# The rest of the largest expert in a mixture-of-experts kernel: first layer with the weights held in the array instead of the tokens

## The chip, the core and the metric

The kernel runs on one core of one Trainium2 chip. A core has TensorE (PE: matrix products, with its weight loads shown apart as PEld), VectorE (DVE), ScalarE (ACT), GpSimd (POOL), SyncE (SP) and 16 DMA engines. The metric is the device time of one execution in microseconds; lower is better.

## The reference

An attention-like first part (no softmax, with a decay mask) makes `x`, 4608 tokens of 512 numbers. A router picks for each token one of 4 groups and in the group one of 4 experts, 16 in all, and each expert is a two-layer network on its own tokens:

```
xg = x[mask_g]
e_idx = np.argmax(xg @ w_expert[g], axis=1)
...
h = np.maximum(xg[mask_e] @ w1[g, e], 0.0)      # [n, 512] @ [512, 1024]
ye = h @ w2[g, e]                               # [n, 1024] @ [1024, 512]
out[tok_idx] = combined[:, None] * ye
```

With the inputs that the reference draws, the two largest experts have 330 tokens each and the smallest 235.

## The kernel before

The attention part fills the first quarter of the span and stores each token's row, with its weight, into a DRAM table `xs` by expert. Then come 17 passes `p`, in the order of the experts' sizes. Pass 0 takes the first 256 tokens of the largest expert (`EARLY`), passes 1 to 15 one expert each, and pass 16 (`E`), which this case is about, the rest of the largest expert: room for 128 tokens (`CS[E]`), of which 330 - 256 = 74 are used.

All 32-bit operands are split in two: `wh` and `xTh` are the rounded part (`fp32r`), `wl` and `xTl` what is left, and a product is three products, high by high, high by low, low by high. A weight piece is a quarter of an expert's first layer or of its second (512 KB each; `load_piece`); `split(k)` makes `wh` on ACT and `wl` on DVE, two instructions each on 128 x 512. Pieces of pass 16 have the numbers `k0` to `k0 + 7`, even ones of the first layer, odd ones of the second.

Passes 1 to 15 go by eight steps `f` of 128 hidden units. `layer1(p, f)` (L593) keeps a 128 x 128 block of weights in the array and streams the tokens past it, 12 matmuls. `layer2(p, f)` (L998 to L1000) does the same, 12 matmuls into four PSUM tiles `py`. `by_width` puts both into a test of the expert's token count on PE: the smaller of two stream lengths is taken where the count allows it (`LOWS[p]`, else `CS[p]`), and both are in the program, behind a branch (L213). Pass 15 streams 238 columns, pass 14 streams 252.

Pass 16 stands behind the loop and is written out by hand. Its first layer (`last1`, L1052) keeps 128 tokens of one 128-row slice of `xT` in the array and streams 256 weight columns: 12 matmuls for each of four pieces. That leaves the hidden units along the free dimension, so `last_tr` (L1063) transposes each piece with two matmuls, after ACT has put it through the ReLU (`hn`), and ACT and DVE split the result into `hhn` and `hln`. Its second layer (`layer2` with `natural(p)`, L987) keeps 128 tokens of `hhn` or `hln` in the array and streams 512 columns of `w2`, three matmuls for each `f`, all into one PSUM tile that has the place of pass 15's `py_0`. `finish` copies this tile on ACT and stores it with one indirect DMA from POOL; `yturn` and `ystore` do the same for pass 15 in eight transposes on DVE and eight DMAs.

Every engine runs its instructions in the order in which the code issues them. `xturn` and `xsplit` make `xTh` and `xTl` of the next pass on DVE and ACT.

Of the kernel before, what the change touches and what calls it, by code (L numbers as in the profile page):

```python
# [7 lines left out]
F32 = mybir.dt.float32  # L8
F32R = mybir.dt.float32r
BF16 = mybir.dt.bfloat16  # L10
I32 = mybir.dt.int32
AF = mybir.ActivationFunctionType
ALU = mybir.AluOpType
AX = mybir.AxisListType

P = 128
# [4 lines left out]
E = G * EG  # L21
NP = H // 2
NKC = DM // P
NFC = F // P
CAPS = [384, 356, 342, 330, 322, 314, 310, 304, 298, 292, 288, 284, 280, 274, 266, 256]
LOWS = [0, 332, 324, 316, 308, 302, 296, 294, 286, 282, 278, 272, 268, 260, 252, 238]
CMAX = CAPS[0]
EARLY = 256
PICK = 26
# [6 lines left out]
NS = N + P  # L36
NT = N // P
NPIECE = 4
# [27 lines left out]
def moe_retention(ctx, tc, qk, kv, wgt, w1, w2, c_f, out):  # L66
# [55 lines left out]
    pe = nc.tensor  # L122
# [35 lines left out]
    def load_piece(i, parts=(0, 1)):  # L158
        if i < len(pieces):
            raws.setdefault(i, []).extend(wload(*pieces[i], part) for part in parts)  # L160
# [9 lines left out]
    def split(k):  # L170
        split_piece(k // 2, k % 2)
# [29 lines left out]
    def width_of(p):  # L201

        wide[p] = nc.values_load(
            sizes[0:1, p : p + 1], engines=[mybir.EngineType.PE], min_val=0, max_val=NS,
            skip_runtime_bounds_check_because="a count of rows, compared only",
        )

# [720 lines left out]
    def rank_experts():  # L928

        key = sm.tile([P, E], F32, name="key")  # L930
        dve.scalar_tensor_tensor(key, cnt, float(E), eid, ALU.mult, ALU.subtract)
        for j in range(2):
            dve.scalar_tensor_tensor(
                key, eah[j], float((2 - j) * BIG), key, ALU.mult, ALU.add
            )
        kk = sm.tile([P, E, E], F32, name="kk", bufs=1)
        ks3 = [P, E, E]
        dve.tensor_tensor(
            kk, key.unsqueeze(1).to_broadcast(ks3), key.unsqueeze(2).to_broadcast(ks3), ALU.is_gt
        )  # L940
        rk = sm.tile([P, E], F32, name="rk")
        dve.tensor_reduce(rk, kk, AX.X, ALU.add)
        dve.tensor_tensor(
            req, rk.unsqueeze(1).to_broadcast(ks3), eid.unsqueeze(2).to_broadcast(ks3), ALU.is_equal
        )
        dve.tensor_tensor(kk, req, eid.unsqueeze(1).to_broadcast(ks3), ALU.mult)
        with nc.allow_low_precision("integers below 16"):
            dve.tensor_reduce(order, kk, AX.X, ALU.add)
        yield

        cr = sm.tile([P, E], F32, name="cr")
        dve.tensor_tensor(kk, req, cnt.unsqueeze(1).to_broadcast(ks3), ALU.mult)
        dve.tensor_reduce(cr, kk, AX.X, ALU.add)
        dve.tensor_copy(sizes[:, 2:], cr[:, 2:])
        dve.tensor_tensor(
            kk[:, :, 0:NB], slb.unsqueeze(1).to_broadcast([P, E, NB]),
            cr.unsqueeze(2).to_broadcast([P, E, NB]), ALU.is_ge,
        )
        dve.tensor_scalar(mia, kk[:, :, 0:NB], float(BIG), None, ALU.mult)
        yield  # L960
        cb, ce = [sm.tile([P, E], F32, name=f"c{x_}", bufs=1) for x_ in "be"]
        dve.tensor_scalar(cb, cr, sln[:, 0:1], None, ALU.add)
        dve.tensor_tensor(ce, cb, cf[:, KC_CAPB : KC_CAPB + E], ALU.is_ge)
        dve.scalar_tensor_tensor(cb, ce, float(E * NS), cb, ALU.mult, ALU.add)
        dve.tensor_copy(ce, order)
        dve.scalar_tensor_tensor(pads, ce, float(NS), cb, ALU.mult, ALU.add)
        el = sm.tile([P, 3], F32, name="el")
        dve.tensor_scalar(el, sln, float(EARLY), None, ALU.add)
        dve.tensor_scalar(mil, el, cr[:, 0:1], float(BIG), ALU.is_ge, ALU.mult)


    def layer2(p, f):
# [33 lines left out]
    def yturn(p, dc, part=0, of=1):  # L1006

        nb = nblocks(p)
        b0, b1 = nb * part // of, nb * (part + 1) // of
        if dc == 0 and part == 0:  # L1010
            ys[p] = mp.tile([P, NB, DQ], F32, name=f"y_{p}", tag="y", bufs=2)
        dve.transpose(
            ys[p][:, b0:b1, 32 * dc : 32 * dc + 32],
            pys[p][dc][:, 32 * b0 : 32 * b1].rearrange("p (b t) -> p b t", t=32),
        )
# [9 lines left out]
    def finish(p, i):  # L1025
# [11 lines left out]
            out_offset=bass.IndirectOffsetOnAxis(ap=iis[p][:n, i : i + 1], axis=0),  # L1037
            in_=y[:n], in_offset=None, bounds_check=N - 1, oob_is_err=False,
        ))

    hns = {}

    def last1(pc):

        wh, wl = wsp[E * NPIECE + pc, 0]
        xh, xl = xTs[E]
        C = CS[E]
        ph = ps_sm.tile([P, 2 * P], F32, name=f"phn_{pc}", tag="sm")
        n = 0
        for kc in range(NKC):  # L1050
            for a, b in ((xh, wh), (xl, wh), (xh, wl)):
                pe.matmul(  # L1052
                    ph[:C], a[:, kc, :C], b[:, kc, :], start=n == 0, stop=n == 3 * NKC - 1
                )
                n += 1
        hns[pc] = mp.tile([P, 2 * P], F32, name=f"hn_{pc}", tag="hn")
        act.activation(hns[pc][:C], ph[:C], AF.Relu)

    def last_tr(pc):
        C = CS[E]  # L1060
        pt = (ps_tr, ps_st)[pc % 2].tile([P, 2, P], F32, name=f"pth_{pc}", tag="tr")
        for i in range(2):
            pe.transpose(pt[:, i, :C], hns[pc][:C, i * P : (i + 1) * P], ident[:C, :C])  # L1063
        hh = mp.tile([P, CMAX], F32R, name=f"hhn_{pc}", tag="hh", bufs=4)
        hl = mp.tile([P, CMAX], F32R, name=f"hln_{pc}", tag="hl", bufs=4)
        hv, lv = [x_[:, : 2 * C].rearrange("p (i c) -> p i c", i=2) for x_ in (hh, hl)]
        act.copy(hv, pt[:, :, :C])
        dve.tensor_tensor(lv, pt[:, :, :C], hv.bitcast(F32), ALU.subtract)
        for i in range(2):
            hts[E, 2 * pc + i] = (hh[:, i * C : (i + 1) * C], hl[:, i * C : (i + 1) * C])  # L1070

    prev = None
    ranks = rank_experts()
    for p in range(E):
        for f in range(NFC):
# [68 lines left out]
                next(ranks, None)  # L1144
            if (p, f) == (0, 6):
                expert_of(2)
            if f == NFC - 3 and p < E - 1:
                width_of(p + 1)
            if (p, f) == (1, 1):
                ids(1)  # L1150
# [17 lines left out]
                ovt = overflow_tables(*ov, mp, phs, cnt, cf, req, ident, ones, pe, dve)  # L1168
            if p in (2, 3):
                next(ovt, None) if (p, f) >= (2, 3) else None  # L1170
            if f == NFC - 3 and p:
                for i in range(3):
                    xturn(p + 1, i, 3)
            if f == NFC - 2 and p:
                for kc in range(NKC):
                    xsplit(p + 1, kc)
            if f == NFC - 1 and 0 < p < E - 1:
# [5 lines left out]


    k0 = 2 * E * NPIECE
    load_piece(E * NPIECE + 3)
    layer2(*prev)
    for part in range(2):
        for dc in range(NKC):
            yturn(E - 1, dc, part, 2)  # L1190
    for b in range(NB):
        ystore(E - 1, b)
    split(k0 + 4)
    last1(0)
    last1(1)
    last_tr(0)
    split(k0 + 6)
    split(k0 + 3)
    last1(2)
    last_tr(1)  # L1200
    layer2(E, 0)
    layer2(E, 1)
    split(k0 + 5)
    last1(3)
    last_tr(2)
    ids(E)
    split(k0 + 7)
    layer2(E, 2)
    layer2(E, 3)
    last_tr(3)  # L1210
    for f in range(4, NFC):
        layer2(E, f)
    finish(E, 0)
    in_order.close()
# [265 lines left out]
```

## Time and profile before

| what | value |
|---|---|
| time, median of 3 runs | 584.69 us (582.01 to 585.03) |
| profiled execution: its time and its span | 583.33 us, 581.5 us |
| PE busy | 565.8 us, 97% of the span, 6045 matmuls |
| PEld busy | 531.1 us, 91% |
| DVE, ACT, POOL busy | 73%, 56%, 44% |
| mean granted clock of TensorE | 0.998 |

The span runs from the first to the last instruction of the profiled execution; its time is 1.8 us more. Busy shares are means over stages with different limits. A matmul's end is modelled, so of PE the starts are what can be read: how far they are apart is what a matmul costs in a stream of them.

### The profile page before, as it was taken

To read this page: it belongs to the slowest core of one execution; us is meant where nothing else is said; L and a number is where in the kernel's file an instruction comes from. 1 tells how busy PE (TensorE), PEld (TensorE's weight loads), DVE (VectorE), ACT (ScalarE), POOL (GpSimd) and SP (SyncE) were. 2 spreads that over 40 slices of the span, in tenths; PEclk is the share of its full clock that TensorE was granted. 3 is DMA by queue.
4 is the path that set the end of the run, shared out by engine and by line. 5 is a ranking of instruction groups with operands and counts; after the bars stand their busy time and mean duration, and the time that the engine had idled before them with its cause. 6 is when DMAs were issued, how large, how long until landed. Compare 5 with 4: busy or idle time off the path is not lost.

```text
span 581.5 us, 16813 instructions
## 1 busy us (share of the span) xinstructions
PE 565.8 (97%) x6045; PEld 531.1 (91%) x6045; DVE 423.7 (73%) x997; ACT 325.8 (56%) x849; POOL 256.5 (44%) x391
## 2 busy tenths in 40 slices
PE   7998999999999999999999999999999999999995
PEld 5887787877768999999999999999999999999994
DVE  4886777878668668876767675867768687687774
ACT  5687877876346545454545454445545455455564
POOL 0022323323323037463645537383644736538465
PEclk9999999999999999999999999999999999999999
DMA  8998998956977952938375665839385684856851
GB/s 327 406 406 320 333 385 300 361 195 187 360 243 295 253 234 63 332 83 311 81 306 155 243 200 195 279 112 342 82 313 160 232 275 141 327 150 243 278 218 42
DMA packets 62410, 141.98 MB, mean 244 GB/s; under 512 B 9425, under 2 KB 30297, under 8 KB 62304
## 3 DMA queue, kind: packets, MB, share of 16 engines
q1 hardware_dynamic: 52944, 120.19, 59.1%
q0 software_dynamic: 9216, 20.28, 9.8%
q8 instruction: 73, 1.20, 0.8%
q14 instruction: 33, 0.27, 0.1%
q10 hardware_dynamic: 144, 0.05, 0.0%
HBM read 120.22 MB, written 24.81 MB: 249 GB/s over the span
## 4 chain that ended last, share of the span: by engine, by line
PE 88%; DVE 4%; DMA 2%; issue 2%; ACT 1%; POOL 1%; SPq 1%; POOLq 0%; DVEq 0%
PE ph L593 33%; PE py L998 11%; PE py L1000 11%; PE py L999 11%; PE px L793 5%; PE pss L749 3%; PE pxt L363 3%; PE px L811 2%; PE pst L778 2%; PE ph L579 2%; PE plt L405 1%; PE py L987 1%; DMA xb<-xs 1%; DMA b<-in_kv 1%; PE pss L737 1%
## 5 line engine op out<-in xcount | busy, mean ns | idle before, releaser
L117 POOL DMA_INDIRECT out<-y,ii x151 | 164.5, 1089 | 62.7 <-issue 30.8
L117 DVE TENSOR_TENSOR wl<-r,wh 128x512 fp32r<-128x512 f32 x260 | 167.4, 685 | 5.5 <-ACT wh L117 2.4
L117 ACT ACTIVATE hh<-ph 128x256 fp32r<-128x256 f32 (+15 forms) x128 | 53.7, 420 | 201.0 <-PE ph L593 136.6
L117 ACT CAST wh<-r 128x512 fp32r<-128x512 f32 x260 | 147.0, 617 | 0.0
L593 PE MATMUL ph<-xTh_m,wh 128*128 128x324 f32 (+16 forms) x488 | 144.9, 297 | 0.0
L593 PE MATMUL ph<-xTl_m,wh 128*128 128x324 f32 (+16 forms) x488 | 144.4, 296 | 0.1
L593 PE MATMUL ph<-xTh_m,wl 128*128 128x324 f32 (+16 forms) x488 | 144.4, 296 | 0.0
L998 PE MATMUL py<-hh,wh 128*128 128x320 f32 (+19 forms) x480 | 142.5, 297 | 0.0
L1000 PE MATMUL py<-hl,wh 128*128 128x332 f32 (+14 forms) x480 | 141.9, 296 | 0.0
L999 PE MATMUL py<-hh,wl 128*128 128x332 f32 (+14 forms) x480 | 141.8, 295 | 0.0
L117 DVE SCALAR_TENSOR_TENSOR hl<-ph,hh 128x256 fp32r<-128x256 f32 (+14 forms) x122 | 57.0, 467 | 95.9 <-ACT hh L117 95.2
L593 PEld LDWEIGHTS ph<-xTl_m,wh 128*128 128x128 f32 x488 | 92.1, 189 | 0.7 <-DVE xTl_m L117 0.4
L593 PEld LDWEIGHTS ph<-xTh_m,wh 128*128 128x128 f32 x488 | 92.1, 189 | 0.4 <-issue 0.2
L593 PEld LDWEIGHTS ph<-xTh_m,wl 128*128 128x128 f32 x488 | 92.2, 189 | 0.0
L999 PEld LDWEIGHTS py<-hh,wl 128*128 128x128 f32 x480 | 90.7, 189 | 0.0
L998 PEld LDWEIGHTS py<-hh,wh 128*128 128x128 f32 x480 | 90.6, 189 | 0.0
L1000 PEld LDWEIGHTS py<-hl,wh 128*128 128x128 f32 x480 | 90.4, 188 | 0.0
L117 POOL COPY pace<-hh 1x1 f32<-1x1 f32 x140 | 30.0, 214 | 132.7 <-ACT hh L117 123.3
L117 POOL DMA_INDIRECT xs<-xt,sl x33 | 32.7, 992 | 109.9 <-DVE xT L117 39.9
L117 ACT ACTIVATE vs<-b,cf 128x64 f32<-128x64 f32 x288 | 72.4, 336 | 7.1 <-DMA b<-in_kv 5.7
L117 DVE TENSOR_TENSOR sT<-pss,masks 128x512 f32<-128x512 f32 x72 | 46.0, 681 | 14.0 <-PE pss L749 7.7
L793 PE MATMUL px<-sT,vs 128*64 128x128 f32 x576 | 39.9, 279 | 0.8 <-issue 0.4
(194 smaller groups left out, 613.0 us busy)
## 6 DMA issues: line engine op xcount, KB each, us to landing
r<-in_w SPq DMA_DIRECT2D x138, 512.0 KB, 7.5
a<-in_qk SPq DMA_DIRECT2D x35, 512.0 KB, 6.4
b<-in_kv SPq DMA_DIRECT2D x31, 512.0 KB
xb<-xs SPq DMA_DIRECT2D x20, 165.0 KB, 3.6
xb<-xs SPq DMA_DIRECT2D x20, 148.5 KB, 3.3
out<-y,ii POOLq DMA_INDIRECT x151, 2.7
xb<-xs SPq DMA_DIRECT2D x12, 181.5 KB, 5.6
b<-in_kv SPq DMA_DIRECT2D x6, 256.0 KB
```

The lines of the kernel that those rows point to most:

```text
L117: i_ = f(*a, **k)
L363: pe.transpose(T["pxt"][:, i, :], T["xT"][:, i, :], ident)
L405: pe.matmul(plt[32 * i : 32 * i + 32], wgp[:, i, :], tiles[t]["xTg"][:, i], start=True, stop=True)
L579: pe.matmul(ph[:, :C], raws[i][0][:, kc, cs], xTf[p][:, kc, :C], start=kc == 0, stop=kc == NKC - 1)
L593: pe.matmul(ph[:, :w], a[:, kc, cs], b[:, kc, :w], start=n == 0, stop=n == 3 * NKC - 1)
L749: pe.matmul(pss[k_, o, (i + par) * P + late * D : (i + par) * P + to], T["kT"][r, i + par, k_], T["qT"][r, i + par, late * D : to], start= ...
L778: pe.matmul(pst[o * D : o * D + D, i, :], T["k"][:, h, :], T["vs"][:, h, :], start=first and i == 0, stop=True, skip_group_check=True,)
L793: pe.matmul(px[g * D : g * D + D, o, s * P : s * P + P], T["vs"][:, 4 * s + 2 * g + o, :], T["sT"][:, o, 2 * s + g, :], start=s == 0, stop ...
L811: pe.matmul(px[g * D : g * D + D, o, s * P + r * w : s * P + r * w + w], st[rows, 2 * s + g, :], T["qT"][rows, 2 * s + g, r * w : r * w + ...
L998: pe.matmul(py[:, :w0], wh[:, f % 2, ds_], hh[:, :w0], start=st_, stop=False)
L999: pe.matmul(py[:, :w], wl[:, f % 2, ds_], hh[:, :w], start=False, stop=False)
L1000: pe.matmul(py[:, :w], wh[:, f % 2, ds_], hl[:, :w], start=False, stop=sp_)
```

## The change

Pass 16 calls the general `layer1` for its first layer: 128 x 128 weights stay in the array and the tokens stream past, 80 columns where the count allows it and 128 else (`LOWS` has a 17th entry, 80). `last1` and `last_tr` go, with the transposes, `hn`, `hhn` and `hln`. The count for the test is 256 less than that of the largest expert, made by one more DVE instruction early on and read by PE in step 5 of pass 15. `xturn` and `xsplit` of pass 16 go from steps 5 and 6 of pass 15 to steps 2 and 3. A second load of the last two weight pieces, which the loop had loaded already, goes. The order behind the loop is written anew.

```
-LOWS = [0, 332, 324, ..., 252, 238]
+LOWS = [0, 332, 324, ..., 252, 238, 80]
...
+        dve.tensor_scalar(sizes[:, 0:1], cr[:, 0:1], float(-EARLY), 0.0, ALU.add, ALU.max)
...
-    def last1(pc):
...
-                pe.matmul(
-                    ph[:C], a[:, kc, :C], b[:, kc, :], start=n == 0, stop=n == 3 * NKC - 1
-                )
...
-    def last_tr(pc):
...
-            pe.transpose(pt[:, i, :C], hns[pc][:C, i * P : (i + 1) * P], ident[:C, :C])
...
-            if f == NFC - 3 and p < E - 1:
+            if f == NFC - 3:
                 width_of(p + 1)
...
-            if f == NFC - 3 and p:
+            if f == (2 if p == E - 1 else NFC - 3) and p:
                 for i in range(3):
                     xturn(p + 1, i, 3)
-            if f == NFC - 2 and p:
+            if f == (3 if p == E - 1 else NFC - 2) and p:
                 for kc in range(NKC):
                     xsplit(p + 1, kc)
...
     k0 = 2 * E * NPIECE
-    load_piece(E * NPIECE + 3)
+    split(k0 + 3)
     layer2(*prev)
-    for part in range(2):
-        for dc in range(NKC):
-            yturn(E - 1, dc, part, 2)
+    for dc in range(NKC):
+        yturn(E - 1, dc, 0, 2)
+    layer1(E, 0)
+    for dc in range(NKC):
+        yturn(E - 1, dc, 1, 2)
     for b in range(NB):
         ystore(E - 1, b)
+    layer1(E, 1)
     split(k0 + 4)
-    last1(0)
-    last1(1)
-    last_tr(0)
+    layer1(E, 2)
+    layer2(E, 0)
+    layer1(E, 3)
     split(k0 + 6)
-    split(k0 + 3)
-    last1(2)
-    last_tr(1)
-    layer2(E, 0)
     layer2(E, 1)
+    layer1(E, 4)
     split(k0 + 5)
-    last1(3)
-    last_tr(2)
+    layer2(E, 2)
+    layer1(E, 5)
     ids(E)
+    layer2(E, 3)
     split(k0 + 7)
-    layer2(E, 2)
-    layer2(E, 3)
-    last_tr(3)
-    for f in range(4, NFC):
+    layer1(E, 6)
+    layer2(E, 4)
+    layer1(E, 7)
+    for f in range(5, NFC):
         layer2(E, f)
     finish(E, 0)
```

On PE, the end of one piece's first layer and what follows it. In a row the streamed operand stands first and the one held in the array second; the shape is that of the stream. Before:

```order
L1052 MATMUL phn_12299<-wh_16_2_12244,xTh_m_12043 128x256
L1052 MATMUL phn_12299<-wh_16_2_12244,xTl_m_12044 128x256
L1052 MATMUL phn_12299<-wl_16_2_12245,xTh_m_12043 128x256
L1063 MATMUL pth_12314<-cf,hn_12278 128x128 x2
L987 MATMUL py_0_12321<-wh_16_0_12082,hhn_12283 128x512
L987 MATMUL py_0_12321<-wl_16_0_12083,hhn_12283 128x512
L987 MATMUL py_0_12321<-wh_16_0_12082,hln_12284 128x512
```

The same place with the change; the rows with 80 columns repeat four times, and 12 rows with 128 columns stand behind the branch.

```order
L213 COMPARE_AND_BRANCH
L593 MATMUL ph_3519<-xTh_m_11840,wh_16_2_12308 128x80
L593 MATMUL ph_3519<-xTl_m_11841,wh_16_2_12308 128x80
L593 MATMUL ph_3519<-xTh_m_11840,wl_16_2_12309 128x80
...
L988 MATMUL py_0_12343<-wh_16_1_12186,hh_3_12347 128x512
L988 MATMUL py_0_12343<-wl_16_1_12187,hh_3_12347 128x512
L988 MATMUL py_0_12343<-wh_16_1_12186,hl_3_12373 128x512
```

Tokens and weights have changed places in the first layer, and the transposes between the layers are gone; the second layer's rows are the same but for their order.

On DVE, behind pass 15: `wl` is the low half of a weight split, `y` pass 15's result on its way out of `py`, `hl` and `hln` the low half of the hidden layer. Before:

```order
L117 TENSOR_TENSOR wl_16_1_12152<-r_16_1_11767,wh_16_1_12151 128x512 x2
L117 STREAM_TRANSPOSE y_12211<-py_0_11730 128x4x32
L117 STREAM_TRANSPOSE y_12211<-py_1_11731 128x4x32
...
L117 TENSOR_TENSOR wl_16_2_12245<-r_16_2_11907,wh_16_2_12244 128x512 x2
L117 TENSOR_TENSOR hln_12284<-pth_12280,hhn_12283 128x256
L117 TENSOR_TENSOR wl_16_3_12288<-r_16_3_12049,wh_16_3_12287 128x512 x2
```

With the change:

```order
L117 TENSOR_TENSOR wl_16_1_12156<-r_16_1_11768,wh_16_1_12155 128x512 x2
L117 TENSOR_TENSOR wl_16_1_12187<-r_16_1_11770,wh_16_1_12186 128x512
L117 STREAM_TRANSPOSE y_12217<-py_0_11731 128x4x32
L117 STREAM_TRANSPOSE y_12217<-py_1_11732 128x4x32
L117 STREAM_TRANSPOSE y_12217<-py_2_11733 128x4x32
L117 STREAM_TRANSPOSE y_12217<-py_3_11734 128x4x32
L117 SCALAR_TENSOR_TENSOR hl_0_12248<-ph_3474,hh_0_12222 128x128
L117 STREAM_TRANSPOSE y_12217<-py_0_11731 128x4x32
L117 SCALAR_TENSOR_TENSOR hl_1_12305<-ph_3519,hh_1_12279 128x128
L117 TENSOR_TENSOR wl_16_2_12309<-r_16_2_11922,wh_16_2_12308 128x512
```

A split of a second-layer piece (`k0 + 3`) now stands ahead of the transposes of `y`, and one instruction on the hidden layer between their two halves.

## Rows read from the trace of the kernel before

**Rows 1.** The page: busy time and share of the span of PE and its weight loads, and the 40 slices of PE and of the granted clock.

```profile
PE 565.8 (97%) x6045; PEld 531.1 (91%) x6045; DVE 423.7 (73%) x997; ACT 325.8 (56%) x849; POOL 256.5 (44%) x391
PE   7998999999999999999999999999999999999995
PEclk9999999999999999999999999999999999999999
```

**Rows 2.** The last stages and two early ones: us from the span's start, length, then for each engine busy us (instructions), the granted clock, DMA share and GB/s.

```profile
4.00:8.00 4.00, 3.35 (x30) 2.50 (x30) 2.23 (x8) 2.01 (x8) 0.00 (x0) 1.00 0.99 358
8.00:12.00 4.00, 2.76 (x45) 2.21 (x44) 2.60 (x5) 2.28 (x9) 0.00 (x0) 1.00 1.04 423
540.00:563.00 23.00, 23.00 (x205) 23.00 (x204) 17.87 (x39) 13.33 (x31) 13.01 (x18) 1.00 0.82 304
563.00:569.00 6.00, 6.00 (x48) 5.78 (x47) 4.78 (x14) 3.33 (x10) 4.13 (x4) 1.00 0.12 38
569.00:575.30 6.30, 6.30 (x36) 5.12 (x34) 4.53 (x11) 3.46 (x9) 4.71 (x5) 1.00 0.13 43
575.30:581.50 6.20, 0.01 (x1) 0.00 (x0) 0.00 (x0) 0.58 (x1) 0.97 (x1) 0.79 0.09 32
```

**Rows 3.** The chain of work that ended last, pieces from 537 us on: start, length, engine, output and line, how many instructions.

```profile
537.28 1.40 PE ph L593 x12
...
548.31 1.35 PE ph L593 x12
...
563.17 2.87 PE phn L1052 x24
566.04 0.22 PE pth L1063 x2
566.25 1.43 PE phn L1052 x12
567.69 0.22 PE pth L1063 x2
567.90 1.39 PE py L987 x6
```

**Rows 4.** The timeline of PE in order of time: start, length, instruction. First a matmul of pass 14 and one of pass 15, then the first matmul and the last of pass 16.

```profile
537.12 0.28 PE L593 MATMUL ph<-xTh_m,wh 128*128 128x252 f32 x1
...
548.15 0.27 PE L593 MATMUL ph<-xTh_m,wh 128*128 128x238 f32 x1
...
563.01 0.28 PE L1052 MATMUL phn<-wh,xTh_m 128*128 128x256 f32 x1
...
574.91 0.40 PE L987 MATMUL py<-wh,hln 128*128 128x512 f32 x1
```

**Rows 5.** Weight loads by shape over the whole span: partitions times columns of the block that is loaded, type, count, then busy us and mean ns of one.

```profile
L405 PEld LDWEIGHTS plt<-xT,wgp 128*32 128x32 f32 x96 | 1.9, 108 | 1.8 <-issue 1.7
L749 PEld LDWEIGHTS pss<-a 64*64 64x64 f32 x896 | 22.3, 133 | 4.8 <-issue 3.7 <-DVE sT L117 0.6
L363 PEld LDWEIGHTS pxt<-cf,xT 128*128 128x128 f32 x144 | 15.3, 140 | 3.5 <-issue 1.3
L593 PEld LDWEIGHTS ph<-xTh_m,wh 128*128 128x128 f32 x488 | 92.1, 189 | 0.4 <-issue 0.2
```

**Rows 6.** The timeline of the weight loads at four places where a load did not wait for the matmul ahead of it to begin: behind a stall, behind a stall, behind two transposes, and behind two transposes.

```profile
177.86 0.19 PEld L987 LDWEIGHTS py<-wh,hh 128*128 128x128 f32 x1 [0.18 <-ACT hh L117]
177.96 0.19 PEld L987 LDWEIGHTS py<-wl,hh 128*128 128x128 f32 x1
...
178.79 0.19 PEld L987 LDWEIGHTS py<-wh,hl 128*128 128x128 f32 x1 [0.64 <-DVE hl L117]
178.90 0.19 PEld L987 LDWEIGHTS py<-wh,hh 128*128 128x128 f32 x1
...
565.99 0.19 PEld L1052 LDWEIGHTS phn<-wh,xTh_m 128*128 128x128 f32 x1
566.09 0.19 PEld L1052 LDWEIGHTS phn<-wh,xTl_m 128*128 128x128 f32 x1
...
572.29 0.19 PEld L987 LDWEIGHTS py<-wh,hhn 128*128 128x128 f32 x1
572.40 0.19 PEld L987 LDWEIGHTS py<-wl,hhn 128*128 128x128 f32 x1
```

**Rows 7.** The timelines of DVE, ACT, POOL and the DMA queue of SP around the end of pass 15 and of pass 16: start, length, instruction, in brackets the idle time ahead of it and what ended it.

```profile
561.49 1.30 DVE L117 TENSOR_TENSOR wl<-r,wh 128x512 fp32r<-128x512 f32 x2
562.77 1.71 DVE L117 STREAM_TRANSPOSE y<-py 128x128 f32<-128x128 f32 x8
...
560.85 2.17 ACT L117 CAST wh<-r 128x512 fp32r<-128x512 f32 x4
575.35 0.58 ACT L117 COPY y<-py 128x512 f32<-128x512 f32 x1 [2.38 <-PE py L987]
...
563.96 0.96 POOL L117 DMA_INDIRECT out<-y,ii  x1 [4.43 <-DVE y L117]
...
573.96 0.97 POOL L117 DMA_INDIRECT out<-y,ii  x1 [0.30 <-issue]
576.21 0.97 POOL L117 DMA_INDIRECT out<-y,ii  x1 [1.28 <-ACTq L1297]
...
540.75 8.94 SPq L117 DMA_DIRECT2D r<-in_w  x12
```

**Rows 8.** DVE's and ACT's groups by shape from 540 to 576 us: count, busy us, mean ns of one, idle time ahead.

```profile
L117 DVE TENSOR_TENSOR wl<-r,wh 128x512 fp32r<-128x512 f32 x28 | 17.9, 684 | 0.6
L117 DVE SCALAR_TENSOR_TENSOR hl<-ph,hh 128x256 fp32r<-128x256 f32 x8 | 3.4, 424 | 4.6 <-ACT hh L117 4.5
L117 DVE TENSOR_TENSOR xTl_m<-xTf,xTh_m 128x128 fp32r<-128x128 f32 x4 | 0.9, 283 | 0.0
...
L117 ACT ACTIVATE hh<-ph 128x256 fp32r<-128x256 f32 x8 | 3.1, 384 | 9.7 <-PE ph L593 7.0 <-POOL pace L117 1.3 <-issue 1.3
L117 ACT CAST xTh_m<-xTf 128x128 fp32r<-128x128 f32 x4 | 0.9, 298 | 0.0
```

More of the change, by code (lines that the diff above doesn't have):

```diff
@@ L25 @@
 CAPS = [384, 356, 342, 330, 322, 314, 310, 304, 298, 292, 288, 284, 280, 274, 266, 256]
-LOWS = [0, 332, 324, 316, 308, 302, 296, 294, 286, 282, 278, 272, 268, 260, 252, 238]
+LOWS = [0, 332, 324, 316, 308, 302, 296, 294, 286, 282, 278, 272, 268, 260, 252, 238, 80]
 CMAX = CAPS[0]
@@ L203, in width_of @@
         wide[p] = nc.values_load(
-            sizes[0:1, p : p + 1], engines=[mybir.EngineType.PE], min_val=0, max_val=NS,
+            sizes[0:1, p % E : p % E + 1], engines=[mybir.EngineType.PE], min_val=0, max_val=NS,
             skip_runtime_bounds_check_because="a count of rows, compared only",
@@ L1039, in finish @@
         ))
-    hns = {}
-    def last1(pc):
[L1045 to L1051, printed above, removed]
-                pe.matmul(
-                    ph[:C], a[:, kc, :C], b[:, kc, :], start=n == 0, stop=n == 3 * NKC - 1
-                )
-                n += 1
-        hns[pc] = mp.tile([P, 2 * P], F32, name=f"hn_{pc}", tag="hn")
-        act.activation(hns[pc][:C], ph[:C], AF.Relu)
-    def last_tr(pc):
-        C = CS[E]
-        pt = (ps_tr, ps_st)[pc % 2].tile([P, 2, P], F32, name=f"pth_{pc}", tag="tr")
-        for i in range(2):
-            pe.transpose(pt[:, i, :C], hns[pc][:C, i * P : (i + 1) * P], ident[:C, :C])
[L1064 to L1070, printed above, removed]
     prev = None
```

## The prediction

> **What bounds the kernel now.** I read the page first: PE is busy for 97% of the span, its weight loads for 91%, and the slices of PE are full to the end [rows 1]. Then the last stages: between 540 and 575.3 us PE has no idle time, and DVE and ACT, which feed it, are busy for 13.3 and 17.9 of 23 us, then for 8 to 9 and for 7 of 12.3 us [rows 2]. The chain of work that ended last says the same: up to the end of pass 16 it runs on PE, matmul behind matmul [rows 3]. Behind PE comes a tail of 6.2 us (575.3 to 581.5) with one ACT copy and one store from POOL [rows 2, 7]. POOL was free at 574.93 and waited 1.28 us for that copy, so POOL does not set the tail; PE's last matmul does. So the change is worth what it does to PE between 563.01 (the first matmul of pass 16) and the last one at 574.91 [rows 4].
>
> **What a matmul costs there.** From the chain: 24 `phn` of 256 columns take 2.87 us, 0.1196 each; two transposes 0.22; six `py` of 512 columns 1.39, 0.232 each [rows 3]. Pass 16 before is 48 x 0.1196 = 5.74, 8 x 0.11 = 0.88 and 24 x 0.232 = 5.56, in sum 12.18 us; the starts give the same (574.91 + 0.23 - 563.01 = 12.13).
>
> **What the change adds and removes on PE.** The second layer keeps its 24 matmuls: 5.56 us. The first layer's 48 + 8 instructions (6.62 us) become 8 x 12 = 96 matmuls, each with a block of 128 x 128 weights of its own and 80 columns to stream: the 74 tokens fit the smaller width. The streamed columns fall from 48 x 256 + 8 x 128 = 13,312 to 7,680, but the loads rise from 56 to 96. So the question is what 96 matmuls cost that load 128 columns and stream 80. No row of before has this shape in the split 32-bit type.
>
> From below: by the stream alone. 512 columns cost 0.232 and 256 cost 0.1196, so 0.00044 a column, and 80 columns would cost 0.1196 - 176 x 0.00044 = 0.042 us.
>
> From above: a load takes 0.189 us from start to end [rows 5]; if nothing of it lay beside other work, a matmul would cost that, 0.189.
>
> Between them stand the rows on the loads themselves. A 32-bit load takes 108 ns for 32 columns, 133 for 64, 189 for 128 [rows 5]: 25 ns for 32 more, 56 for 64 more, so some 100 to 112 ns of the 189 grow with the columns, and the rest is a delay that the next load can share. The four places of [rows 6] show exactly that. Normally a load starts as the matmul ahead of it starts, and one can't see what the load alone needs. At these four it starts later than that, because the load before it is in the way, and there two loads start 0.10, 0.11, 0.10 and 0.11 us apart, while each takes 0.19. The streams are no counter-example: 252 columns cost 1.40 / 12 = 0.1167 and 238 cost 1.35 / 12 = 0.1125 [rows 3, 4], never under what the loads need. I read it so: loads of 128 columns of 32 bits can't follow each other faster than some 0.105 us, pass 15 already runs just above that, and a shorter stream buys nothing more. I take 0.109, halfway between the 0.105 of the loads and the 0.1125 that was seen in a long stream.
>
> So 96 x 0.109 = 10.46, with the second layer 16.02, against 12.18: **PE needs 3.84 us more.** With 0.10 it is 2.98 more, with 0.1125 it is 4.18.
>
> **A rule of the skill against the row.** The Trainium skill, "TensorE: Matmul & The Clock Gate", section "Back-to-back issue gap", gives about 81 ns a matmul for a sustained stream of load and matmul at 128 columns. By it the first layer would take 96 x 0.081 = 7.8 us and pass 16 some 1.2 us more than now. Against it, for this type, stand [rows 6]; what it would do here is the first rival's upper part.
>
> **What else moves, costed at nothing.** *Splits.* ACT and DVE must deliver, and PE is slower now, so they have time. Walked through with a split at 1.13 us on ACT (four casts took 2.17 [rows 7]) and 1.29 on DVE, a hidden layer at no more than 0.38 and 0.42 [rows 8]: DVE ends `wl` of `k0 + 2` at 562.79 [rows 7], of `k0 + 3` at 564.1, the first half of `y` (four of the eight transposes, 0.86) at 564.9, `hl_0` at 565.3, the second half at 566.2. The first `py` of pass 16 needs that PSUM tile and is due behind three first layers, at 563.01 + 36 x 0.109 = 566.9: 0.7 us to spare. The next splits: `k0 + 4` is ready at 567.9 and due at 569.6, `k0 + 6` at 571.2 and due at 573.6, `k0 + 5` at 573.2 and due at 574.9, `k0 + 7` at 575.2 and due at 577.6. If one comes late, PE waits by that much; nothing else is behind it but the end. *Steps 2 and 3 of pass 15* get the turn and split of pass 16's tokens: step 3 has `hl` 0.42, `wl` 1.29 and four `xTl` 0.89 on DVE, 2.6 of the 2.70 us that a step takes on PE (twice 1.35 [rows 3]), and ACT 0.38 + 1.13 + 0.90. It is what step 6 has now without a gap on PE, and `hl` is needed only one first layer (1.35 us) later. Uncovered it would cost 0.9. *Loads.* Two loads of 512 KB go, the last of twelve issued from 540.75 on [rows 7]. DMA is at 0.12 of its time behind 563 [rows 2], PE waits for none of them: nothing. The pieces are all issued before 550 as before. *Tests.* Eight more tests of the width on PE and one more read of a count. Each step of pass 15 has two of them and PE has no gap there [rows 2]: nothing. *Stores.* POOL's eight stores of pass 15 start about 1 us later (564.9 for 563.96), take 11 us and end near 576, and the last store is due behind 579.7: nothing. The tail behind PE stays at 6.2 us.
>
> **The sum** goes against the profiled execution's own time: 583.33 + 3.84 = 587.2. That execution was 1.4 us under the median of the three runs and inside their spread; from the median it is 588.5. I forecast the middle, **587.9 us**. What a measurement of this kernel tells from no change is about 0.5%, 2.9 us; 3.84 is 0.66%.
>
> **Rivals.**
>
> *The loads hide (not slower).* The loads of [rows 6] may be late for another reason, and short streams let them run faster; the transposes speak for it, whose loads take 140 ns for the same 128 columns [rows 5]. At 0.042 a matmul, PE reaches the first `py` at 563.01 + 36 x 0.042 = 564.5, but DVE frees the tile only at 566.2: a wait of 1.6 us takes part of the gain. 4.03 + 5.56 + 1.6 = 11.2, 1.0 us less than now: 582.3 to 583.7. At 0.081 it is 13.3 and a wait of 0.3, 1.4 us more: 584.8 to 586.1. The point from which it decides is the distance of two loads: below 0.1 us the change is not slower by 0.5%. Against it stand all four places. 0.11.
>
> *Load and stream don't overlap at 80 columns (much slower).* A load that waits until the short stream is out: 0.109 + 0.042 = 0.15 a matmul, 14.4 in all, 7.8 us more: 591 to 592.5; with the whole 0.189, 18.1 and 11.5 more: 595 to 596. Against it: matmuls and loads lie beside each other in every long stream. 0.05.
>
> *The granted clock falls in pass 16.* The array would stream for some 0.03 to 0.04 of every 0.109 us. The mean granted clock was 0.79 behind the last matmul, where PE did nothing [rows 2], so idle time does lower it to 1.2 from 2.4 GHz; but it stayed at 1.00 where PE had nothing in flight for 0.65 and 1.24 of 4 us [rows 2]. No row has matmuls of this type at the lower level; with everything on PE twice as long the bound is 16 us, 604. 0.04.
>
> **Chances.** My forecast 0.80, the hidden loads 0.11, no overlap 0.05, the clock 0.04. Most of the forecast's own spread is that of the runs, 1.5 us to each side, so some of it falls under the 2.9 us: slower 0.70, within 0.5% 0.27, faster 0.03 (the hidden loads at their best, with a low median). The likeliest case alone holds 586.3 to 588.9; the range for 8 in 10, with the spread of the runs and a part of the rivals, is 585.0 to 591.0.
>
> **What would show it.** In the changed kernel, pass 16's `ph` on L593 with 80 columns start 0.108 to 0.112 us apart, 12 in about 1.31 us, and each load starts as the one ahead is through; PE's stretch from the first matmul of pass 16 to the last grows from 12.1 to about 16 us without a gap, and the tail behind it stays at 6.2. Wrong would be: `ph` less than 0.1 us apart; a gap on PE before the first `py` that DVE's `y` ends; a gap in steps 3 to 5 of pass 15; a granted clock under 1.00 ahead of the last matmul.

## The result and the profile after

The changed kernel is slower: the ratio of its times to those of the kernel before, measured on the same chip, is **1.0073, 95% interval 1.0050 to 1.0096** (14 executions of each). On the 583.17 us median of before in that comparison this is +4.3 us, where +3.84 was predicted. Of the 14 executions of the changed kernel, 4 took 597 to 602 us at a mean granted clock of 0.971 to 0.978: the ratio leaves them out, the median of all 14, 589.16 us (584.65 to 602.07), holds them, and E4, E5 and E8 to E10 are about them. The profiled execution took 585.17 us, its span 583.4.

The page after: busy time of PE and its loads, and the 40 slices of PE and of the granted clock, for [rows 1].

```profile
PE 567.6 (97%) x6085; PEld 533.8 (92%) x6085; DVE 424.5 (73%) x1002; ACT 325.3 (56%) x849; POOL 256.1 (44%) x391
PE   7998999999999999999999999999999999999995
PEclk9999999999999999999999999999999999999999
```

Forty more matmuls (6085 for 6045) and no other sign: at this distance the two pages look alike. The windows cut at the first and behind the last matmul of pass 16 show the difference, first of before, then of the changed kernel (columns as in [rows 2]).

```profile
540.00:563.01 23.01, 23.01 (x206) 23.01 (x205) 17.88 (x40) 13.34 (x31) 13.01 (x18) 1.00 0.82 304
563.01:575.14 12.13, 12.13 (x82) 10.89 (x80) 9.30 (x24) 6.79 (x17) 8.84 (x8) 1.00 0.13 41
575.14:581.50 6.36, 0.17 (x1) 0.00 (x0) 0.00 (x0) 0.58 (x1) 0.97 (x1) 0.79 0.09 31
```

```profile
540.00:560.76 20.76, 20.76 (x187) 20.76 (x185) 16.45 (x36) 12.44 (x29) 13.05 (x18) 1.00 0.73 276
560.76:577.04 16.28, 16.28 (x122) 15.04 (x120) 10.19 (x28) 6.32 (x16) 8.44 (x8) 1.00 0.10 33
577.04:583.40 6.36, 0.17 (x1) 0.00 (x0) 0.00 (x0) 0.59 (x1) 0.97 (x1) 0.80 0.08 29
```

PE is busy without a gap in both, from 540 us on and through pass 16. Pass 16 takes 16.28 for 12.13 us, **+4.15**, and the tail behind it 6.36 in both. The whole span is only 1.9 us longer, because in this one execution pass 16 began 2.25 us earlier, at 560.76 for 563.01. The program ahead of that point moves by as much from one execution to the next: in the traces of this case, pass 16 began between 560.8 and 566.1 us. So kernels are compared here by the stretch of pass 16, and by the ratio of many times.

The chain of work that ended last, for [rows 3]: the 36 matmuls of three first layers, one piece's second layer, the next first layer, its second layer.

```profile
560.92 3.95 PE ph L593 x36
564.87 0.78 PE py L988 x3
565.65 1.26 PE ph L593 x12
566.91 0.77 PE py L988 x3
...
567.84 0.30 issue
568.14 1.16 POOL out L117
```

3.95 / 36 = 0.1097 us a matmul of 80 columns. At 567.84, in the middle of pass 16, the view leaves PE and follows POOL's stores to the end. In the trace of before it does so at 569.43, behind the pieces that [rows 3] show:

```profile
569.43 0.30 issue
569.74 0.97 POOL out L117
```

So this view alone doesn't show that PE sets the end. The rows of the end do: POOL's last store waits for ACT's copy of the result (4.73 us after, in the POOL rows further down; 1.28 before [rows 7]), and the copy waits for PE's last matmul (2.38 us before [rows 7]), after:

```profile
577.25 0.59 ACT L117 COPY y<-py 128x512 f32<-128x512 f32 x1 [1.88 <-PE py L988]
```

The timeline of PE at the start of pass 16, at its first `py` and at its end, for [rows 4]:

```profile
560.76 0.20 PE L593 MATMUL ph<-xTh_m,wh 128*128 128x80 f32 x1
560.79 0.28 PE L593 MATMUL ph<-xTl_m,wh 128*128 128x80 f32 x1
560.90 0.28 PE L593 MATMUL ph<-xTh_m,wl 128*128 128x80 f32 x1
...
564.58 0.28 PE L593 MATMUL ph<-xTh_m,wl 128*128 128x80 f32 x1
564.69 0.48 PE L988 MATMUL py<-wh,hh 128*128 128x512 f32 x1
565.01 0.40 PE L988 MATMUL py<-wl,hh 128*128 128x512 f32 x1
...
576.81 0.40 PE L988 MATMUL py<-wh,hl 128*128 128x512 f32 x1
```

In the stream they start 0.11 us apart. The first of a group is an exception (0.03 ahead of the second: its load starts at 560.65, under the 238-column stream before it), and the first `py` behind a group has the other side of it (0.32 to the next in place of 0.23). Over a group the two cancel: 12 distances of 0.1115 and 3 of 0.232 make 2.03 us, eight times that 16.3.

### The profile page after: what moved, and what is told of

It is laid out like the page before. It is cut to its first block, busy times and chain, and to the rows that moved or that the text cites. A ratio compares the mean times of both kernels' runs of the same rounds, so it can differ in the third digit from the quotient of the medians.

```text
span 583.4 us, 16906 instructions
## 1 busy us (share of the span) xinstructions
PE 567.6 (97%) x6085; PEld 533.8 (92%) x6085; DVE 424.5 (73%) x1002; ACT 325.3 (56%) x849; POOL 256.1 (44%) x391
## 4 chain that ended last, share of the span: by engine, by line
PE 85%; DVE 5%; DMA 4%; issue 2%; ACT 1%; POOL 1%; SPq 1%; POOLq 0%; DVEq 0%; ACTq 0%
PE ph L593 34%; PE py L999 11%; PE py L1001 11%; PE py L1000 11%; PE px L793 4%; PE pss L749 3%; PE pxt L363 3%; DMA b<-in_kv 3%; PE px L811 2%; PE pst L778 2%; PE ph L579 2%; PE plt L405 1%; PE py L988 1%; DMA xb<-xs 1%; DVE sT L117 1%
## 5 line engine op out<-in xcount | busy, mean ns | idle before, releaser
L117 ACT ACTIVATE hh<-ph 128x256 fp32r<-128x256 f32 (+16 forms) x136 | 56.1, 412 | 208.9 <-PE ph L593 143.4
L593 PE MATMUL ph<-xTh_m,wl 128*128 128x316 f32 (+17 forms) x520 | 153.5, 295 | 0.0
L593 PE MATMUL ph<-xTh_m,wh 128*128 128x316 f32 (+17 forms) x520 | 153.5, 295 | 0.0
L593 PE MATMUL ph<-xTl_m,wh 128*128 128x316 f32 (+17 forms) x520 | 153.4, 295 | 0.0
L117 DVE SCALAR_TENSOR_TENSOR hl<-ph,hh 128x256 fp32r<-128x256 f32 (+15 forms) x130 | 59.3, 456 | 100.0 <-ACT hh L117 99.3
L593 PEld LDWEIGHTS ph<-xTl_m,wh 128*128 128x128 f32 x520 | 98.2, 189 | 0.8 <-DVE xTl_m L117 0.3
L593 PEld LDWEIGHTS ph<-xTh_m,wh 128*128 128x128 f32 x520 | 98.2, 189 | 0.5 <-issue 0.2
L593 PEld LDWEIGHTS ph<-xTh_m,wl 128*128 128x128 f32 x520 | 98.3, 189 | 0.0
(178 smaller groups left out, 579.8 us busy)
```

The source lines that it names most:

```text
L117: i_ = f(*a, **k)
L593: pe.matmul(ph[:, :w], a[:, kc, cs], b[:, kc, :w], start=n == 0, stop=n == 3 * NKC - 1)
```

## The experiments

Ratios are to the kernel before on the same chip and in the same set of runs; its median was 585.22 us in the first set (E1 to E4), 587.48 in the second (E5 to E7) and 584.32 in the third (E8 to E10). So medians are compared within a set. The sets ran on different chips, and the changed kernel itself was not run in the second and the third.

### E1: the moved work alone

The kernel before, with the turn and split of pass 16's tokens in steps 2 and 3 of pass 15, the split of piece `k0 + 3` ahead, and without the doubled load; first layer as before.

```
-            if f == NFC - 3 and p:
+            if f == (2 if p == E - 1 else NFC - 3) and p:
...
-            if f == NFC - 2 and p:
+            if f == (3 if p == E - 1 else NFC - 2) and p:
...
-    load_piece(E * NPIECE + 3)
+    split(k0 + 3)
...
-    split(k0 + 3)
```

> The kernel before, first layer of pass 16 as it was (tokens in the array, transposes), with the rest of the change alone: turn and split of pass 16's tokens in steps 2 and 3 of pass 15, the split of k0 + 3 ahead of the transposes of y, no second load of the last two pieces. If the loads of the first layer are the whole cost, this is as fast as before: 0 us, at most 0.3 to either side, and the stretch of pass 16 on PE is 12.1 to 12.2 us. If the new placing costs or gains something, it shows here: up to 0.9 us slower for an uncovered token split, up to 1.3 us slower if the late transposes of y hold back the first py.

Measured: 584.79 us, ratio 0.9994 (0.9965 to 1.0024). The windows of its pass 15 and pass 16:

```profile
540.00:564.61 24.61, 24.61 (x220) 24.61 (x218) 19.52 (x44) 14.79 (x35) 13.04 (x18) 1.00 0.69 247
564.61:576.74 12.13, 12.13 (x82) 10.90 (x80) 9.34 (x24) 6.84 (x16) 7.95 (x8) 1.00 0.13 41
```

No gap in pass 15 and the same 12.13 us in pass 16: the moved work costs and gives nothing that shows here. What is left for the difference is the first layer's new form, with its tests and its order.

### E2: three times the columns, the same loads

```
+                    if p == E:
+                        pe.matmul(
+                            ph[:, : 3 * w].rearrange("p (a w) -> p a w", a=3), a[:, kc, cs],
+                            b[:, kc, :w].unsqueeze(1).to_broadcast([P, 3, w]), start=n == 0, stop=n == 3 * NKC - 1
+                        )
+                        n += 1
+                        continue
```

> The changed kernel with each 80-column stream of pass 16's first layer sent three times in one matmul, into 240 PSUM columns of which the first 80 are used: three times the streamed columns, the same 96 loads. If the load sets the cost, a matmul stays at 0.111 to 0.114 us, and the kernel at the changed one's time, +0.1 to +0.3 us. If the streamed columns set it, 160 more columns at 0.00044 us are 0.07 us a matmul, 96 of them 6.7 us more than the changed kernel. If short streams cost extra by a lower granted clock, this one has none of that and is faster than the changed kernel by what the clock took.

Measured: 589.34 us, ratio 1.0069 (1.0041 to 1.0097). PE at the start of pass 16:

```profile
563.04 0.27 PE L594 MATMUL ph<-xTh_m,wh 128*128 128x240 f32 x1
563.15 0.27 PE L594 MATMUL ph<-xTl_m,wh 128*128 128x240 f32 x1
```

The pass takes 16.37 us. 160 columns more in each of 96 matmuls cost 0.09 us in all: below 240 columns the stream is not what is paid.

### E3: a third of the loads less

For `wh`, one stream of 160 columns in place of the two of the high and the low part of the tokens, and 80 columns for `wl`: 64 loads for the same 7,680 columns. The 160 columns are the high part twice over, so the kernel leaves out the product of the low part.

```
+                if p == E:
+                    pe.matmul(
+                        ph[:, : 2 * w].rearrange("p (a w) -> p a w", a=2), wh[:, kc, cs],
+                        xh[:, kc, :w].unsqueeze(1).to_broadcast([P, 2, w]), start=n == 0, stop=False
+                    )
+                    pe.matmul(ph[:, :w], wl[:, kc, cs], xh[:, kc, :w], start=False, stop=n == 3 * (NKC - 1))
+                    n += 3
+                    continue
```

> The changed kernel with 64 in place of 96 loads for the same streamed columns: the two matmuls that share a block of weights are one with 160 columns. It leaves out the product of the low part of the tokens with the weights (the high part is streamed twice in its place), so that its output is not exact. If the load sets the cost, 32 matmuls less at 0.111 us: 3.6 us faster than the changed kernel, 0.4 to 0.6 us slower than before. If the streamed columns set it, the same time as the changed kernel.

Measured: 584.75 us, ratio 0.9999 (0.9980 to 1.0019). Pass 16:

```profile
561.77:574.46 12.69, 12.69 (x90) 11.47 (x88) 9.54 (x28) 6.23 (x16) 8.51 (x8) 1.00 0.12 39
```

16.28 - 12.69 = 3.59 us for 32 loads, 0.112 each, at the same columns. This is the whole loss of the change but for half a microsecond. E3 takes 32 matmuls away together with their loads; E2 shows that it is not their columns, and E6 and E7 below keep the number of matmuls and make the loads alone cheaper. Together they show that the loads set the pass.

### E4: the changed kernel once more

No edit.

> The changed kernel itself beside the three others on one chip: 4.0 to 4.3 us slower than before, the stretch of pass 16 on PE 16.2 to 16.4 us for 12.1.

Measured: 589.23 us (587.26 to 601.61), ratio 1.0062 (1.0024 to 1.0101), pass 16 at 16.28 us. Two of seven executions took 599.9 and 601.6 us, at a mean clock of 0.971 and 0.977.

### E5: the first layer twice

```
+            if p == E:
+                by_width(p, sums)
             by_width(p, sums)
```

> The changed kernel, with the first layer of pass 16 run twice over (its sums are simply started anew; the result is the same): 192 instead of 96 matmuls of 80 columns, each with a block of 128 x 128 weights. Theory (one load every 0.1115 us sets the pass, whatever stretch it fills): pass 16 on PE goes from 16.28 to 16.28 + 96 x 0.1115 = 27.0 us, the kernel is 10.7 us slower than the changed one, and the granted clock stays at 1.00 ahead of the last matmul. Rival (the granted clock falls where the array streams for only a third of the time, and 10.7 us of such matmuls were just not long enough to show it): the clock is under 1.00 in the second half of the pass, the matmuls there stand more than 0.1115 us apart, and the whole is more than 11.5 us slower than the changed kernel.

Measured: 620.87 us (619.17 to 623.61), ratio 1.0571 (1.0542 to 1.0600), far over what 96 loads more cost. The theory on the loads doesn't cover it; the rival does. Windows of PE alone (length, busy time, granted clock, DMA), and two places of the timeline:

```profile
570.75:571.00 0.25, 0.25 (x4) 1.00 0.47 164
571.00:571.25 0.25, 0.25 (x4) 0.90 0.31 99
571.25:571.50 0.25, 0.25 (x4) 0.50 0.00 0
...
571.60:612.60 41.00, 40.96 (x169) 0.51 0.03 9
```

```profile
566.07 0.20 PE L593 MATMUL ph<-xTh_m,wh 128*128 128x80 f32 x1
...
580.24 0.41 PE L593 MATMUL ph<-xTh_m,wl 128*128 128x80 f32 x1
580.45 0.41 PE L593 MATMUL ph<-xTh_m,wh 128*128 128x80 f32 x1
```

At 571.2, 5.1 us behind the first short matmul, the clock falls to 0.50, 1.2 GHz, although PE has not been idle for a moment since the pass began. It stays there until 612.2, the start of the last of the nine 512-column matmuls that end the pass, with `ph` 0.21 us apart. The pass takes 46.5 us.

### E6: the same matmuls in 16 bits

```
+                    if p == E:
+                        a16 = a[:, kc, cs].bitcast(BF16)[:, 1 : 2 * P : 2]
+                        b16 = b[:, kc, :w].bitcast(BF16)[:, 1 : 2 * w : 2]
+                        pe.matmul(ph[:, :w], a16, b16, start=n == 0, stop=n == 3 * NKC - 1)
+                        n += 1
+                        continue
```

> The changed kernel, with the 96 matmuls of pass 16's first layer reading only the upper 16 bits of each number of both operands, as bf16 (every second 16-bit word of the same tiles); so the split's precision is left out there, and the number of loads, their 128 x 128 shape and the 80 columns stay. Theory (the 0.1115 us are the price of a load of 32-bit weights): the matmuls stand closer than 0.1115 us, between the 0.056 of a load of half the bytes and 0.10; pass 16 is between 11 and 15.3 us on PE, and the kernel 1 to 5 us faster than the changed one. Rival (the distance belongs to the pair of load and matmul whatever its type): 0.111 us apart, 16.3 us on PE, the time of the changed kernel. The Trainium skill, 'TensorE: Matmul & The Clock Gate', section 'Back-to-back issue gap', gives 0.081 us for a matmul with its load at 128 columns; by it this run would be 96 x 0.03 = 2.9 us faster than the changed kernel.

Measured: 590.56 us, ratio 1.0050 (1.0030 to 1.0070). The distance of the matmuls and the time of the pass answer differently:

```profile
564.32 0.20 PE L596 MATMUL ph<-xTl_m,wh 128*128 128x80 bf16 x1
564.36 0.20 PE L596 MATMUL ph<-xTh_m,wl 128*128 128x80 bf16 x1
564.39 0.20 PE L596 MATMUL ph<-xTh_m,wh 128*128 128x80 bf16 x1
...
566.03 0.47 PE L994 MATMUL py<-wh,hh 128*128 128x512 f32 x1 [0.82 <-DVE y L117]
...
571.64 0.50 PE L994 MATMUL py<-wh,hh 128*128 128x512 f32 x1 [0.53 <-ACT wh L117]
...
577.70 0.51 PE L994 MATMUL py<-wh,hh 128*128 128x512 f32 x1 [1.97 <-ACT hh L117]
```

```profile
563.72:579.66 15.94, 11.51 (x122) 7.82 (x120) 9.76 (x28) 6.12 (x16) 8.89 (x8) 0.97 0.10 33
```

At 0.037 us apart the matmuls are three times as fast as with 32 bits, below even the expected 0.056: the 0.1115 us belong to the 32-bit type, and since E2 rules the stream out, to the load. But the pass still takes 15.94 us, since PE now stands idle for 4.4 of them. The brackets name for what: VectorE's transposes of pass 15's result, a split of weights on ACT, and ACT's `hh` of the last pieces; another 0.7 us stand inside one group of short matmuls, and the profile names nothing for them. By the starts the loss is larger, 6.6 us over distances of 0.037 and 0.232 us, most of it (5.8) at these places. My expectation of 1 to 5 us less forgot these waits.

### E7: half the columns in each load

```
+                    if p == E:
+                        half = slice(cs.start, cs.start + 64)
+                        pe.matmul(ph[:64, :w], a[:, kc, half], b[:, kc, :w], start=n == 0, stop=n == 3 * NKC - 1)
+                        n += 1
+                        continue
```

> The changed kernel, with the 96 matmuls of pass 16's first layer loading only the first 64 of their 128 weight columns; half of the hidden layer of that pass is left out so, the 80 streamed columns and the number of loads stay. Theory (a load's price goes with the columns that it loads): 0.056 us apart, or somewhat more, the first layer 5.4 instead of 10.7 us; pass 16 on PE about 11 us, or up to 12.4 if PE then waits for VectorE's transposes of pass 15's result before its first py; the kernel 4 to 5 us faster than the changed one, and as fast as the one before or up to 1.2 us faster. Rival (each load has a fixed price of 0.11 us, and the columns only add to its delay): 0.11 us apart, the time of the changed kernel.

Measured: 590.66 us, ratio 1.0064 (1.0042 to 1.0087). Again the rows and the time differ:

```profile
565.24 0.23 PE L595 MATMUL ph<-xTl_m,wh 128*64 128x80 f32 x1
565.30 0.23 PE L595 MATMUL ph<-xTh_m,wl 128*64 128x80 f32 x1
...
578.63 0.50 PE L993 MATMUL py<-wh,hh 128*128 128x512 f32 x1 [1.94 <-ACT hh L117]
```

```profile
564.69:580.36 15.67, 12.98 (x122) 10.19 (x120) 9.76 (x28) 6.12 (x16) 8.88 (x8) 0.98 0.11 34
```

0.06 us apart for 64 columns, against 0.11 for 128: the price of a 32-bit load goes with the columns that it loads, as the theory has it. (The kernel leaves out half of the hidden layer of pass 16.) The time doesn't follow, for E6's reason: by the starts 4.4 us are lost over distances of 0.058 and 0.232 us, with 2.7 us of idle PE, 1.94 of them ahead of one `py` that waits for ACT's `hh`. What holds ACT up there (it stands idle for 1.6 us, and the trace names no work of this core as the cause) was not found out. One of the 12 executions took 596.89 us at a mean clock of 0.987; no trace of it was taken.

The clock of 0.97 and 0.98 in these two passes comes from their ends: behind the wait of 1.97 and 1.94 us PE starts again at 577.70 and 578.63, and at 578.7 and 579.8 the clock falls to 0.50, under the last matmuls. It costs 0.2 to 0.5 us here.

### E8 to E10: how many short streams stand in a row

In the changed kernel 36 matmuls of 80 columns stand ahead of the first `py`, 4.0 us. E8 makes them 48, E9 24, E10 leaves 36 and makes them 240 columns wide.

E8:

```
     layer1(E, 2)
+    layer1(E, 3)
     layer2(E, 0)
-    layer1(E, 3)
```

> The changed kernel, with the fourth first layer of pass 16 put ahead of its first second layer: 48 matmuls of 80 columns in a row (5.3 us) instead of 36 (4.0 us); the work is the same. Theory (the granted clock falls when PE runs long enough on short streams alone: it fell 5.5 us after the first of them where there were 72 in a row, and stayed at 1.00 in the profiled execution with 36): here it falls in most executions, the profile shows 0.50 for a part of pass 16, the pass takes 20 to 32 instead of 16.3 us and the kernel 5 to 16 us longer than the changed one. Rival (the fall with 72 in a row came of the doubled work as a whole, not of the stretch without long streams): clock 1.00 through the pass, 16.3 us, the time of the changed kernel.

E9:

```
     split(k0 + 4)
+    layer2(E, 0)
     layer1(E, 2)
-    layer2(E, 0)
     layer1(E, 3)
```

> The changed kernel, with its first second layer of pass 16 put ahead of the third first layer: at most 24 matmuls of 80 columns in a row (2.7 us). Theory: the clock stays at 1.00 in pass 16 in all executions, none has a mean clock near 0.975; PE waits 0.2 to 0.6 us for VectorE's transposes of pass 15's result, so the pass takes 16.4 to 16.9 us and the kernel as long as the changed one or up to 0.6 us longer. Rival (the order does not bear on the clock): as with the changed kernel, more than one execution in four is some 10 to 13 us above the others, at a mean clock near 0.975.

E10 is E2's edit with `if p == E and f < 3:`.

> The changed kernel, with each of the 36 streams ahead of the first second layer sent three times over in one matmul (240 columns, the further two copies not read by anything); the other 60 stay at 80 columns. Theory (a load sets 0.11 us for 80 and for 240 columns alike, and a long stream keeps the clock up): pass 16 takes 16.3 to 16.4 us at clock 1.00, and no execution has a mean clock near 0.975. Rival (short streams in groups of 12 between second layers are enough for the fall): some executions are 8 to 13 us above the others, at a mean clock near 0.975.

| kernel | short streams in a row | executions at a mean clock of 0.980 or less | time of these | median of all |
|---|---|---|---|---|
| E9 | 24 | 0 of 12 | - | 587.89 us |
| E10 | 36, 240 columns wide | 0 of 12 | - | 589.18 us |
| changed kernel (both sets) | 36 | 6 of 21 | 597.4 to 602.1 us | 589.16 and 589.23 us |
| E8 | 48 | 6 of 12 | 595.9 to 600.0 us | 594.53 us |
| E5 | 72 | 6 of 6 | 619.2 to 623.6 us | 620.87 us |

E2, with all its streams at 240 columns, has none in 7, the kernel before none in 25, 18 and 29 of its executions; of the 14 in the first comparison only the times are on record, the longest 585.94 us. The line is drawn at 0.980 because a short fall early in the span takes something off the mean too: in E4's trace (mean 0.994) the clock is 0.86 between 95 and 100 us, where PE is busy for 3.36 of 5 us, and 1.00 in pass 16. The profiled execution of E8 shows where the time goes; windows of PE alone, and then the pass cut at the fall:

```profile
565.75:566.00 0.25, 0.25 (x5) 1.00 0.16 49
566.00:566.25 0.25, 0.25 (x5) 0.90 0.00 0
566.25:566.50 0.25, 0.25 (x3) 0.50 0.00 0
```

```profile
562.03:566.20 4.17, 4.17 (x41) 4.17 (x39) 3.67 (x13) 1.59 (x5) 1.81 (x2) 1.00 0.07 24
566.20:588.95 22.75, 22.75 (x84) 20.10 (x83) 6.59 (x16) 4.71 (x12) 6.19 (x7) 0.50 0.06 19
```

4.17 us behind the first short matmul the clock falls (E8's expectation has 5.5 us for E5, from a coarser window; by the finer ones it is 5.1), with PE busy throughout, and stays at 0.50 for the 22.75 us that are left: 26.92 us for the pass, 10.6 more than with the clock at 1.00. By time and mean clock it fell in half of the executions, where I had expected most. E9 has the same work in another order and its pass takes 16.28 us at 1.00, without the wait that I had expected:

```profile
564.28:580.56 16.28, 16.28 (x122) 15.04 (x120) 10.29 (x28) 6.32 (x16) 8.43 (x8) 1.00 0.10 33
```

E10's takes 16.32. So order and width bear on the fall, as the theory has it. The firmest comparison is that of E8 with E9 and with E10, on one chip: 6 of 12 against 0 of 12, which chance alone gives less than once in a hundred times. Against the changed kernel's 6 of 21, which come from other sets, 0 of 12 would come by chance about once in twenty. What decides in one execution and not in another with 36 or 48 in a row was not looked into. The ratios, taken as in the section on the result, are 1.0099 (1.0059 to 1.0139) for E8, 1.0076 (1.0048 to 1.0105) for E9 and 1.0075 (1.0043 to 1.0108) for E10, and the medians of E9 and E10 are 3.6 and 4.9 us above that of before: without the fall, the loss to the loads is still there. No trace was taken of one of the six long executions of the changed kernel; that its clock fell in pass 16 is concluded from their time and clock, which are those of E8.

## Why the prediction was right, and where it was not

**The time.** The forecast was 587.9 us, 585.0 to 591.0; measured were 589.16. The ten executions at the higher clock have a median of 588.1, so 1.1 of the 1.3 us between come from the other four, which the forecast's sum has no term for.

**PE sets the end.** Right: the tail behind PE's last matmul is 6.36 us in both kernels, cut at the same point, and the ratio follows the pass on PE (+4.15 us in the profiled executions, +4.3 by the ratio). Two readings under it were wrong. The chain does not run on PE up to the end of pass 16: it leaves PE at 569.43, and it is the waits at the end that show PE's part. And between 540 and 563 us it is DVE that is busy for 17.87 us and ACT for 13.33 [rows 2], not the other way round; nothing hangs on that.

**Pass 16 before.** The sum of 12.18 and the 12.13 from the starts are both what the windows give, 12.13.

**96 loads of 0.109 us.** The mechanism is right and was shown from two sides: three times the columns at the same loads change nothing (E2), a third fewer loads give 3.59 us back (E3), and loads of fewer columns or bits let the matmuls closer (E7, E6). The size was a little small. (16.28 - 5.56) / 96 = 0.1117, close to the upper of the values that I had weighed (0.1125, of the 238-column stream) and not the middle; 96 x 0.0027 = 0.26 us is what separates 16.28 from the predicted 16.02. The four distances of [rows 6], 0.10 to 0.11, lie just under it; why a stream doesn't keep the shorter ones was not looked into.

**The rule that I set against the row** gave 0.081 us a matmul and so +1.2 us; the row was right, 0.111. The Trainium skill has a nearer rule that I had not weighed: "TensorE: Matmul & The Clock Gate", section "LDWEIGHTS (loading the stationary operand)", gives columns / 1.2 ns for a load, that is an estimate of 107 ns for 128 columns and 53 for 64, whatever the number of partitions. The runs agree to 5 and 10%: 0.1115, and 0.058 in E7 (33 distances from 564.77 to 566.70). The Trainium skill, same page, section "Weight-path perf modes — Fast Weight Load (FWL) and DoubleRow", has a faster load for 128 columns of a type that is not FP32; E6's 0.037 us agrees in kind.

**Splits, steps 2 and 3, dropped loads, tests, stores at nothing.** Right. E1 shows it apart from the rest for the steps, the loads and the early split; for the tests and the stores there is only that PE has no gap after. The walk through DVE's splits holds when it is moved by the 2.25 us by which pass 16 began earlier: the rows of DVE and POOL after,

```profile
562.79 0.90 DVE L117 STREAM_TRANSPOSE y<-py 128x128 f32<-128x128 f32 x4
...
564.43 1.29 DVE L117 TENSOR_TENSOR wl<-r,wh 128x512 fp32r<-128x512 f32 x2 [0.22 <-ACT wh L117]
...
562.81 0.97 POOL L117 DMA_INDIRECT out<-y,ii  x1 [5.50 <-DVE y L117]
...
578.11 0.97 POOL L117 DMA_INDIRECT out<-y,ii  x1 [4.73 <-ACT y L117]
```

for [rows 7], have `y` done at 563.69 (predicted 566.2 - 2.25 = 563.95), the first `py` at 564.69 (564.65), and the split of `k0 + 4` done at 565.72 (565.65). POOL's eight stores start at 562.81, and it is idle for 4.73 us ahead of the last one.

**The rival in which the loads hide** did not come, and its price was wrong as well. I had put a pass with cheap loads at 11.2 to 13.6 us and named 0.1 us as the point below which the change would not be slower. E6 and E7 have cheap loads, 0.037 and 0.058 us, and their pass takes 15.94 and 15.67 us: they are as slow as the changed kernel. I had counted one wait, that for `y`, and "if one comes late, PE waits by that much" stood only in the part on the slow loads. The later waits for splits and `hh` cost more than the first. In the changed kernel PE waits for no split: with the loads at 0.11 us they are all done in time.

**The rival of the clock** was the miss. I gave it 0.04, on the ground that the clock had stayed at 1.00 in windows in which PE had nothing in flight for 0.65 and 1.24 of 4 us [rows 2], and put it at 604 us. The profiled execution has 1.00 through the pass, as forecast. But 6 of 21 executions took 597 to 602 us, and E5 and E8 show in their traces that a row of short streams brings the clock down while PE is never idle. That is one of the prediction's own signs of being wrong, a granted clock under 1.00 ahead of the last matmul. The step that failed is the one from idle time of PE to the clock: [rows 2] show stretches in which PE has nothing in flight, and say nothing on a row of short streams without a gap. The Trainium skill, same page, section "HAM oscillation — how this bites in real kernels", ties the fall to gaps in which PE is idle; here it fell without one, at 566.2 in E8, and the measurement decides. The prediction of the time held since most executions escaped; that nearly three in ten would not was worth a place in the spread. Over all 14 executions the mean is 591.04 us for 583.46 before, +7.6 us: with the falls, the change costs nearly twice what the loads alone take.

## What to carry to other kernels

Count loads before columns: with 32-bit operands of 128 x 128 a matmul costs what its load costs, 0.11 us here, until its stream is some 240 columns long, so making the few tokens the streamed side trades cheap columns for dear loads. When a bound is lifted in thought, walk the whole chain of the next engine's due times and not the first one: E6 and E7 had matmuls that would make the pass 7 and 5 us shorter by their distances, and came out no faster. And spread short streams between long ones: the same work in E9's order has none of 12 executions at a mean clock of 0.980 or less, where the changed kernel has 6 of 21 and E8's order 6 of 12.

## What the runs showed of the hardware

- The granted clock fell from 2.4 to 1.2 GHz with PE busy all the time, 4.2 (E8) and 5.1 us (E5) behind the first of a row of 80-column matmuls 0.11 us apart, and did not come back while short and long streams alternated, for 22.75 and 41 us. In E5 it came back behind eight matmuls of 512 columns in a row; in E8 nine of them end the pass, and it stayed down. With the first 36 matmuls at 240 columns, equally far apart, none of 12 executions had a mean clock of 0.980 or less (E10).
- At the lower clock both kinds of matmul stand nearly twice as far apart: those of 80 columns 0.21 us in E5 for 0.11, those of 512 columns 0.43 in E8 for 0.23.
- A load of 128 columns of 32 bits costs 0.111 us in a stream, one of 64 columns 0.058 (E7), one of 128 columns of 16 bits no more than 0.037 (E6), all three with 80 streamed columns.
